# Seven block products instead of eight in part of the in-projection of a gated-attention and MLP kernel

## The chip, the cores and the metric

One core of a Trainium2 chip runs the kernel. The metric is the device time of one execution in microseconds. Its engines are called PE (TensorE, matrix products), DVE (VectorE), ACT (ScalarE), POOL (GpSimd) and SP (SyncE, which issues the DMAs); PEld is PE's loading of weights.

## What is computed

```
def _attn_ref(q, k, v, alpha):              # 4 batches, 8 heads, 768 tokens, 48 wide
    for t in range(S):
        state = alpha[:, :, t, :, None] * state + einsum('bhd,bhe->bhde', k[:, :, t], v[:, :, t])
        y[:, :, t] = einsum('bhd,bhde->bhe', q[:, :, t], state)

def _moe_ref(x, w_gate, w_val, w_out, rms_g):   # x: 3072 tokens x 384, d_ff 1536
    rms = np.sqrt(np.mean(x * x, axis=-1, keepdims=True) + 1e-06)
    xn = x / rms * rms_g
    g = xn @ w_gate
    silu = g * (1.0 / (1.0 + np.exp(-g)))
    val = xn @ w_val
    return (silu * val @ w_out).astype(np.float32)
```

Gated linear attention goes first; its output, laid out by token, is x of the gated MLP.

## The kernel before

All products have fp32 accuracy: each operand is kept as a high and a low half in fp16, and a product is the sum of three matmuls (SPLIT: high x high, high x low, low x high). ACT makes a high half, DVE subtracts it to get the low one.

The 3072 tokens are 24 chunks of 128. `attention(cc)` does a chunk: decays by a scan on DVE, scores (L753), masking, the state (L926), the output y in one PSUM tile (L832, L853), RMS norm, and a transpose by DMA into xT. Chunks make up GROUPS = [4, 2, 2, 4, 4, 4, 4], so groups 5 and 6, with which the change deals, have 512 tokens each.

The MLP's in-projection goes by group g and block f of 128 out of d_ff (12 blocks). `expert_in` (L1154) computes such a unit: two outputs, gate and value, each the sum over NK = 3 blocks of k and three splits, nine matmuls of 512 columns into a PSUM bank `bk` of its own. Then ACT takes silu of the gate (L1165), DVE multiplies by the value (L1171), ACT makes the high half of h (L498) and DVE the low one (L1188). The out-projection of groups 0 to 4 is `expert_out` (L1473, 384 columns). Groups 5 and 6 (SEVEN) already have an out-projection by seven block products in place of eight, `expert_out7` (L1355, 192 columns), with the sums of h (`combine`, L1255 to L1271) and of the weights (`combine_w`, L1293 to L1310) on DVE.

The order is written out: every piece of work of every engine is an op of `Plan`, and ORDER is a table of op numbers. `Plan.order()` goes through it with planned costs, chooses the buffers and lists each engine's ops by their planned start. Each engine then works its list strictly in order. Up to a planned time of 45 us the planner puts filler matmuls (`warm`, L1593, 512 columns, results unused) into gaps that it foresees on PE. There are six PSUM banks `bk` and one tile `y` of two banks for the attention's output. The tile layer adds the semaphores: an access of a tile waits for the accesses of other engines to that tile which it must follow.

## Time and profile before

| | |
|---|---|
| median of 3 runs | 499.30 us (499.09 to 499.84) |
| the profiled execution | 498.64 us, its span 496.8 us |
| PE busy | 489.6 us, 99% of the span |
| DVE busy | 421.5 us, 85% |
| ACT busy | 276.4 us, 56% |

The page gives busy times of each engine over the span; the windows give the same for stretches that follow the stages: group 0's in-projection runs from 28 to 80 us, group 1 from 107, group 2 from 150, group 3 from 192, group 4 from 274; group 5's in-projection from 354 to 402 with its out-projection up to 424; group 6's in-projection from 424 to 470 and its out-projection from there to 492. A recorded matmul or DVE instruction is longer than the distance to the next one's start in a full row, so lengths and distances are told apart in what follows.

### The profile page before, as it was taken

The numbers are of one execution on the slowest core, as the hardware profiler recorded it, in microseconds if no ns is written. First come the engines' busy times: TensorE is split into PE (matmuls) and PEld (weight loads), VectorE is DVE, ScalarE is ACT, GpSimd is POOL, SyncE is SP. The second block draws the span as 40 slices with busy tenths as digits, with TensorE's granted clock in tenths as the row PEclk, the third lists the DMA queues.
The fourth block names the chain that finished last, engine by engine and source line by source line (L and its number), as shares of the span: only waits on it lengthen the run. The fifth ranks groups of instructions, "written<-read, shape, count | busy, mean of one in ns | idle before, by whom it ended". The sixth has DMA issues, their size and how long they took to land.

```text
span 496.8 us, 12664 instructions
## 1 busy us (share of the span) xinstructions
PE 489.6 (99%) x5200; PEld 311.1 (63%) x5200; DVE 421.5 (85%) x822; ACT 276.4 (56%) x751; POOL 27.3 (5%) x63
## 2 busy tenths in 40 slices
...
GB/s 306 311 198 198 296 227 193 164 144 134 112 138 211 58 92 190 73 165 35 34 290 221 322 150 144 144 206 223 55 26 2 33 1 42 7 17 1 2 1 84
DMA packets 47042, 65.22 MB, mean 131 GB/s; under 512 B 32641, under 2 KB 39042, under 8 KB 46978
## 3 DMA queue, kind: packets, MB, share of 16 engines
...
## 4 chain that ended last, share of the span: by engine, by line
PE 58%; issue 33%; DVE 5%; POOL 2%; ACT 1%; POOLq 0%; DVEq 0%; ACTq 0%
PE bk L1154 34%; PE bk_po L1473 10%; PE bk_ab L1355 6%; PE bk_d L1355 2%; POOL ss L958 2%; PE bk L753 2%; DVE w L646 1%; PE y L853 1%; PE bk_warm L607 1%; PE warm L1593 1%; PE bk L926 1%; PE y L832 1%; DVE h L1171 0%; DVE a L883 0%; DVE kh L676 0%
## 5 line engine op out<-in xcount | busy, mean ns | idle before, releaser
L1154 PE MATMUL bk<-xT,wg 128*128 128x512 f16 (+1 forms) x1602 | 286.5, 338 | 0.1
L1154 PEld LDWEIGHTS <-wg 128*128 128x128 f16 x1602 | 154.4, 98 | 120.4 <-issue 0.6
L1473 PE MATMUL bk_po<-wo,h 128*128 128x384 f16 x576 | 96.9, 326 | 0.0
L1473 PEld LDWEIGHTS <-h 128*128 128x128 f16 x576 | 55.0, 98 | 35.6
L498 ACT ACTIVATE h<-h 128x512 f16<-128x512 f32 (+1 forms) x89 | 45.8, 515 | 40.0 <-DVE h L1171 40.0
L1171 DVE SCALAR_TENSOR_TENSOR h<-bk,sl 128x512 f32<-128x512 f32 (+1 forms) x89 | 51.2, 580 | 17.9 <-PE bk L1154 14.8
L1165 ACT ACTIVATE sl<-bk 128x512 f32<-128x512 f32 (+1 forms) x89 | 44.8, 508 | 38.4 <-PE bk L1154 35.9
L646 DVE TENSOR_TENSOR_SCAN w<-att,seed 112x520 f32<-112x520 f32 x48 | 59.3, 1235 | 2.1 <-DMA att<-att 1.7
L1188 DVE TENSOR_TENSOR h<-h,h 128x256 f16<-128x256 f32 (+1 forms) x89 | 47.4, 543 | 6.4 <-ACT h L498 6.3
L958 POOL TENSOR_TENSOR ss<-ss,mhalf 128x1 f32<-128x1 f32 x24 | 21.4, 890 | 383.6 <-ACT ss L955 383.6
L880 ACT CAST a<-bk 128x512 f16<-128x512 f32 x40 | 23.0, 581 | 29.7 <-DVE bk L769 29.6
L883 DVE TENSOR_TENSOR a<-bk,a 128x512 f16<-128x512 f32 x40 | 26.8, 682 | 2.3 <-ACT a L880 2.2
L769 DVE TENSOR_TENSOR bk<-bk,mask 128x512 f32<-128x512 f32 x40 | 26.9, 690 | 2.1 <-PE bk L753 2.1
L683 DVE TENSOR_TENSOR qp<-att,w 112x256 f32<-112x256 f32 x48 | 19.4, 418 | 0.2
L1355 PEld LDWEIGHTS <-h 128*128 128x128 f16 x216 | 17.9, 98 | 0.5 <-issue 0.2
L753 PEld LDWEIGHTS <-k 48*128 48x128 f16 x480 | 13.4, 94 | 6.8 <-issue 6.5
L995 ACT ACTIVATE x<-x,ss 128x384 f16<-128x384 f32 x20 | 12.2, 611 | 9.1 <-issue 4.0
L498 ACT ACTIVATION_READ_ACCUMULATOR h<-h 128x1 f32 x89 | 16.9, 190 | 0.0
L753 PE MATMUL bk<-q,k 48*128 48x128 f16 x480 | 16.9, 217 | 0.0
L676 DVE TENSOR_TENSOR kh<-att,w 112x512 f32<-112x512 f32 x24 | 16.4, 683 | 0.0
L853 PEld LDWEIGHTS <-a 128*128 128x128 f16 x368 | 13.8, 96 | 3.1 <-DVE a L883 0.3
L998 DVE SCALAR_TENSOR_TENSOR x<-x,ss,x 128x384 f16<-128x384 f32 x20 | 12.2, 610 | 3.6 <-ACT x L995 3.5
...
## 6 DMA issues: line engine op xcount, KB each, us to landing
...
```

The costliest lines, as they stand in the source:

```text
L498: nc.scalar.activation(dst, src, AF.Copy, scale=scale, accum_out=stat[:rows, col : col + 1])
L646: nc.vector.tensor_tensor_scan(w, x, start.rearrange("r g p c -> r (g p c)"), 0.0, op0=ALU.mult, op1=ALU.add)
L753: nc.tensor.matmul(t["sc"][j][:, p, :], t["k16"][r, x, p, :], t["q16"][r, y, p, :], start=m == 0, stop=m == 2,)
L769: nc.vector.tensor_tensor(t["sc"][j], t["sc"][j], mask.to_broadcast([P, NP, C]), op=ALU.mult)
L883: nc.vector.tensor_tensor(a_tile()[:, j, 1], t["sc"][j], a_tile()[:, j, 0], op=ALU.subtract)
L958: nc.gpsimd.tensor_tensor(t["ss"], t["ss"], mhalf, op=ALU.pow)
L1154: nc.tensor.matmul(ps[:, :n], wg[:, f, x, j, kk, :], xT[:, y, kk, cs], start=i == 0, stop=i == 3 * NK - 1,)
L1165: nc.scalar.activation(t["sl"][:, :n], t[0][:, :n], AF.Silu, scale=1.0 / (S_X * S_W))
L1171: nc.vector.scalar_tensor_tensor(t["h"][:, :n], t[1][:, :n], S_H / (S_X * S_W), t["sl"][:, :n], op0=ALU.mult, op1=ALU.mult,)
L1188: nc.vector.tensor_tensor(lo, used(t["h"][:, :n]), hi, op=ALU.subtract)
L1355: nc.tensor.matmul(bank(b), left(n, x, p), right(n, y, p), start=begin and p == 0 and m == 0, stop=end and p == n2 - 1 and m == 2, skip_gr ...
L1473: nc.tensor.matmul(t[i][:, :DM], h16_of(g, f)[:, x, ts], wo[:, f // 2, y, f % 2, :], start=f == 0 and m == 0, stop=f == NF - 1 and m == 2,)
```

## The change

Sixteen units, blocks 4 to 9 of group 5 and 0 to 9 of group 6, go through a new function `expert_in7`. Of a unit, the gate and value outputs, two halves of the tokens (256 each) and two of the three blocks of k form a product of 2x2 block matrices. It is made of seven block products, each three matmuls of 256 columns, with sums of weight blocks and of x blocks in place of some operands; the third block of k is added as before (12 matmuls of 256). The partial sums lie in two `bk` banks, `a` and `e`, and in a tile `y_late`, made of the two banks that the attention's y held: yb in its first bank, yd in its second, each with places for two units.

- PE: 1 (into a), 5 (into e), 6 (a), 7 (a), then 2 with third (yb), 4 with third (a), 3 with third (e), third (yd).
- ACT copies a three times on the way: to yb behind 1 (`fork`), to SBUF as u2 behind 6 (`second`) and as u3 behind 7 (`next_`).
- DVE adds e and u3 to yd (`jd`) and later e and u2 to u2 (`jc`); gate and silu come in halves of 256.
- `combine_in` forms the weights' sums, for five pairs of blocks, and `combine_x` those of x, for the two groups: an addition of 1024 columns, four of 256, a copy of the high halves on ACT and a subtraction on DVE. The results lie in four new tiles wi, or in buffers lent by the attention.
- `set_bits` writes y_late once with two matmuls of 512 columns, so that all later products into it accumulate.
- The attention's last chunks and the checks of the weights are now listed ahead of group 5's in-projection.
- The planner has costs for the new ops, counts yb and yd as two buffers each, and lets an access of a PSUM bank start only when other engines' planned accesses of that bank are done (`bank_of`).
- The whole ORDER table is another one. The scratch size for dynamic DMAs is set to 1024. In the changed kernel old lines stand 21 lower at first (L1154 is L1175, L1171 is L1192), and 272 to 281 lower towards the end (L1355 is L1627, L1593 is L1874).

```diff
+WINO = range(10)
+WINO_OF = {5: range(4, 10), 6: range(10)}
...
-    xT=2, raw=2, wu=2, h16=13, sl=2, h32=3, ob=2, bk=6, y=1,
+    xT=2, raw=2, wu=2, h16=13, sl=2, h32=3, ob=2, bk=6, y=1, yb=2, yd=2,
...
 ORDER = """
-1 0 7 8 9 a 2 c d 4 5 b e u x f g y 39 3b 3 v h i j z 3a 6 10 3c 12 13 k l 11 14 3d 3e 15 n o 1k 1m 17
...
+0 1 4 5 2 7 8 9 a b c d u x 6 z h i e f v y g 10 39 11 12 3b 3a 13 3c 3d 14 15 1k 1m 3e 1n 3 1p 1q 17 j
...
+    def bank_of(self, k):
+        return (k[0], self.slot[k]) if k[0] == "bk" else k[0] if k[0] in ("yb", "yd") else None
...
+                for x, f in bank.get(self.bank_of(k), {}).items():
+                    if x != e:
+                        t = max(t, f)
...
+        def form(w):
+            w = w.rearrange("p (f n c) -> p f n c", f=len(fs), n=4)
+            a11, a12, a21, a22 = [w[:, :, n] for n in range(4)]
+            nc.vector.tensor_tensor(a22, a21, a22, op=ALU.add)
+            nc.vector.tensor_tensor(a21, a11, a21, op=ALU.subtract)
+            nc.vector.tensor_tensor(a11, a22, a11, op=ALU.subtract)
+            nc.vector.tensor_tensor(a12, a12, a11, op=ALU.subtract)
...
+        def bank(k):
+            if k[0] == "bk":
+                return tile_of(k, lambda: buf(ps_bk, [P, 512], F32, *k))[:, :n]
+            i = plan.slot[k]
+            return y_late[0][:, 0 if k[0] == "yb" else 1, i * n : (i + 1) * n]
...
+        def product(o, p, start=False):
+            for m, (x, y) in enumerate(SPLIT):
+                nc.tensor.matmul(o, left(p, x), right(p, y), start=start and m == 0, stop=m == 2, skip_group_check=True)
+
+        def third(o, j, c):
+            for m, (x, y) in enumerate(SPLIT):
+                nc.tensor.matmul(
+                    o, wg[:, f, x, j, 2, :], xT_of(g)[:, y, 2, c * n : (c + 1) * n], start=False, stop=m == 2,
+                    skip_group_check=True,
+                )
...
+        p1 = add("PE", "pw", lambda: product(bank(k_a), 1, True), deps, [x_k, k_a])
+        p5 = add("PE", "pw", lambda: product(bank(k_e), 5, True), [p1, w_op, *x_s], xs_k + [k_e] + w_keys)
+        fk = add("ACT", "fork", fork, [p1, y_bits[0]], [k_a, k_b])
+        p6 = add("PE", "pw", lambda: product(bank(k_a), 6), [fk, w_op, *x_s], xs_k + [k_a] + w_keys)
+        u2 = add("ACT", "fork", second, [p6], [k_a, k_2])
+        p7 = add("PE", "pw", lambda: product(bank(k_a), 7), [u2], xs_k + [k_a] + w_keys)
+        u3 = add("ACT", "fork", next_, [p7], [k_a, k_3])
+        jd = add("DVE", "jn", lambda: join(lambda: bank(k_d), lambda: t["u3"]), [u3, p5, y_bits[0]], [k_e, k_d, k_3])
+        b = add("PE", "pw2", lambda: p_third(lambda: bank(k_b), 2, 0, 0), [fk], [x_k, k_b])
+        c = add("PE", "pw2", lambda: p_third(lambda: bank(k_a), 4, 1, 0), [u3], xs_k + [x_k, k_a])
+        e = add("PE", "pw2", lambda: p_third(lambda: bank(k_e), 3, 0, 1), [jd], [x_k, k_e] + w_keys)
+        d = add("PE", "pw", lambda: third(bank(k_d), 1, 1), [jd], [x_k, k_d])
+        tail[0] = d
+        last_unit[g] = [c, e, d]
+        s0 = op("ACT", IN_COST[2][1], lambda: silu(0), [b], [k_b, s_k])
+        jc = add("DVE", "jn", lambda: join(lambda: t["u2"], lambda: t["u2"]), [e, u2], [k_e, k_2])
+        s1 = op("ACT", IN_COST[2][1], lambda: silu(1), [jc, s0], [k_2, s_k])
+        h0 = op("DVE", IN_COST[2][2], lambda: gate(0), [c, s0], [k_a, s_k, h_k])
+        h1 = op("DVE", IN_COST[2][2], lambda: gate(1), [d, s1, h0], [k_d, s_k, h_k])
...
+            y_late.append(buf(ps_y, [P, 2, 512], F32, "y", "late"))
+            for j in range(2):
+                nc.tensor.matmul(
+                    y_late[0][:, j].rearrange("p (o c) -> p o c", o=4), minus,
+                    minus.rearrange("p (o c) -> p o c", o=1).to_broadcast([P, 4, P]), start=True, stop=True,
+                )
...
+        if g == SEVEN[0]:
+            for cc in range(starts[g] + m, NC):
+                xt_ops[cc] = attention(cc)
+            check_weights()
+            set_bits()
+            for f in WINO[::2]:
+                combine_in(WINO[f : f + 2])
+        if g in SEVEN:
+            combine_x(g, [xt_ops[starts[g] + i] for i in range(m)] + last_unit.get(g - 1, []))
...
-            expert_in(g, f, c0, c1, deps)
+            if f in WINO_OF.get(g, ()):
+                expert_in7(g, f, deps)
+            else:
+                expert_in(g, f, c0, c1, deps)
```

Three places show what the new table does to the engines' lists. The first is PE near the start of the program. Before, behind the scores of chunk 0 (bk_0_0 and bk_0_1) and its sums along the chunk (bk_0_4), four warm matmuls come ahead of chunk 0's output y_0:

```order
L763 MATMUL bk_0_1_202<-qp_0_190,kh_0_199 64x64 x2
L890 MATMUL bk_0_4_225<-one_115,kh_0_199 128x112 [waits PE_49,Pool_49]
L890 MATMUL bk_0_4_225<-one_115,kh_0_199 128x112 x3
L1593 LDWEIGHTS minus_112
L1593 MATMUL warm_232<-minus_112 128x512
L1593 LDWEIGHTS minus_112
L1593 MATMUL warm_232<-minus_112 128x512
...
L1593 LDWEIGHTS minus_112
L1593 MATMUL warm_232<-minus_112 128x512
L790 MATMUL y_0_246<-v_0_170,a16_0_230 64x48 [waits DMAHW5_49,DVE_49]
L790 MATMUL y_0_246<-v_0_170,a16_0_230 64x48
```

After, the sums stand ahead of the scores, and 19 warm matmuls follow in a row, the first of them waiting for ACT; then come the scores of chunk 1 and three more warm ones, and chunk 0's output only behind them:

```order
L784 MATMUL bk_0_1_208<-qp_0_197,kh_0_195 64x64 x2
L784 MATMUL bk_0_0_207<-qp_0_197,kh_0_195 64x64 x2
L784 MATMUL bk_0_1_208<-qp_0_197,kh_0_195 64x64 x2
L1874 LDWEIGHTS minus_112
L1874 MATMUL warm_229<-minus_112 128x512 [waits Activation_49]
...
L1874 MATMUL warm_229<-minus_112 128x512
L784 MATMUL bk_1_0_266<-qp_1_260,kh_1_257 64x64 [waits DVE_49]
L784 MATMUL bk_1_0_266<-qp_1_260,kh_1_257 64x64
...
L911 MATMUL bk_1_4_284<-one_115,kh_1_257 128x112 [waits PE_49]
L1874 LDWEIGHTS minus_112
L1874 MATMUL warm_296<-minus_112 128x512
L811 MATMUL y_0_305<-v_0_177,a16_0_249 64x48 [waits DMAHW7_49]
```

What moved: chunk 1's scores went ahead of chunk 0's output, and the long row of fillers stands ahead of them.

The second is PE in group 5's in-projection, around block 4 (bk_5_4 is its bank, xT the tokens, wg the weights). Before, one output's nine matmuls of 512 columns follow the other's, and the next block comes behind:

```order
L1154 MATMUL bk_5_4_0_1_6426<-xT_5_5143,wg_143 128x512
L1154 LDWEIGHTS wg_143
L1154 MATMUL bk_5_4_0_1_6426<-xT_5_5143,wg_143 128x512
L1154 LDWEIGHTS wg_143
L1154 MATMUL bk_5_5_0_0_6441<-xT_5_5143,wg_143 128x512 [waits DVE_49]
L1154 LDWEIGHTS wg_143
L1154 MATMUL bk_5_5_0_0_6441<-xT_5_5143,wg_143 128x512
```

After, the pieces are of three matmuls of 256 columns or six, blocks 4 to 6 are interleaved, and here product 7 of block 4 (weights' sums wi2 and x sums q16_X), product 1 of block 6 and product 2 of block 4 into yb follow each other:

```order
L1396 LDWEIGHTS wi2_147
L1396 MATMUL bk_5_4_a_6478<-q16_X_5_0_6282,wi2_147 128x256 [waits Activation_49]
...
L1396 LDWEIGHTS wi2_147
L1396 MATMUL bk_5_4_a_6478<-q16_X_5_0_6282,wi2_147 128x256
L1396 LDWEIGHTS wg_143
L1396 MATMUL bk_5_6_a_6565<-xT_5_5161,wg_143 128x256 [waits DVE_49]
L1396 LDWEIGHTS wg_143
...
L1396 LDWEIGHTS wg_143
L1396 MATMUL y_late_6469<-xT_5_5161,wg_143 128x256 [waits DVE_49]
L1396 LDWEIGHTS wg_143
L1396 MATMUL y_late_6469<-xT_5_5161,wg_143 128x256
```

What moved: three destinations within nine matmuls, and each of the three pieces begins with a wait, for ACT or for DVE, where before a piece waited only for its bank to come free.

The third is DVE at the same place (h32 is h, h16 its halves, raw_S sums of h). Before, block 5's gate (L1171) is followed by the sums of blocks 4 and 5 for the out-projection:

```order
L1188 TENSOR_TENSOR h16_5_2_6470<-h32_5_2_0_6337,h16_5_2_6470 128x2x128 [waits Activation_49]
L1271 TENSOR_TENSOR att_S_5_1_6472<-raw_S_5_1_6421,att_S_5_1_6472 128x1024 [waits Activation_49]
L1171 SCALAR_TENSOR_TENSOR h32_5_5_0_6491<-bk_5_5_0_1_6459,sl_5_5_0_6476 128x512 [waits DVE_49,PE_49,Activation_49]
L1255 TENSOR_TENSOR raw_S_5_2_6493<-h32_5_4_0_6451,h32_5_5_0_6491 128x256 [waits DVE_49]
L1256 TENSOR_TENSOR raw_S_5_2_6493<-h32_5_4_0_6451 128x256
L1257 TENSOR_TENSOR raw_S_5_2_6493<-raw_S_5_2_6493,h32_5_4_0_6451 128x256 [waits DVE_49]
L1258 TENSOR_TENSOR raw_S_5_2_6493<-h32_5_5_0_6491,raw_S_5_2_6493 128x256 [waits DVE_49]
L1171 SCALAR_TENSOR_TENSOR h32_5_6_0_6522<-bk_5_6_0_1_6500,sl_5_6_0_6510 128x512 [waits PE_49,Activation_49]
```

After, the low halves (L1209) of blocks 2 and 3 come ahead of the joins (L1420) of blocks 5 and 4 into y_late, with the sums of the weights of blocks 8 and 9 (L1284 to L1292) in between; kT_U is u2 and x16_U is u3:

```order
L1209 TENSOR_TENSOR h16_5_2_6529<-h32_5_2_0_6521,h16_5_2_6529 128x2x128 [waits Activation_49]
L1209 TENSOR_TENSOR h16_5_3_6550<-h32_5_3_0_6538,h16_5_3_6550 128x512 [waits Activation_49]
L1420 TENSOR_TENSOR y_late_6469<-bk_5_5_e_6540,x16_U_5_5_6559 128x256 [waits PE_49,Activation_49]
L1284 TENSOR_TENSOR raw_L_w_8_6580<-wg_143 128x1024
L1420 TENSOR_TENSOR y_late_6469<-bk_5_4_e_6531,x16_U_5_4_6569 128x256 [waits DVE_49,Activation_49]
L1289 TENSOR_TENSOR raw_L_w_8_6580<-raw_L_w_8_6580 128x2x128 [waits DVE_49]
L1290 TENSOR_TENSOR raw_L_w_8_6580<-raw_L_w_8_6580 128x2x128 [waits DVE_49]
L1291 TENSOR_TENSOR raw_L_w_8_6580<-raw_L_w_8_6580 128x2x128 [waits DVE_49]
L1292 TENSOR_TENSOR raw_L_w_8_6580<-raw_L_w_8_6580 128x2x128 [waits DVE_49]
L1420 TENSOR_TENSOR kT_U_5_4_6544<-bk_5_4_e_6531,kT_U_5_4_6544 128x256 [waits PE_49]
L1420 TENSOR_TENSOR kT_U_5_5_6527<-bk_5_5_e_6540,kT_U_5_5_6527 128x256
L1265 TENSOR_TENSOR v16_W_7_1_6524<-raw_L_w_6_6472,v16_W_7_0_6523 128x512
```

What moved: joins, which PE's next products wait for, now stand in one list with sums that only later units need.

## Rows read from the trace of the kernel before

**Rows 1.** The page: the span, and busy time of each engine.

```profile
span 496.8 us, 12664 instructions
PE 489.6 (99%) x5200; PEld 311.1 (63%) x5200; DVE 421.5 (85%) x822; ACT 276.4 (56%) x751; POOL 27.3 (5%) x63
```

**Rows 2.** Windows: stretch, length, busy us of each engine, PEclk, DMA share, GB/s.

```profile
core 0: us, PE busy (x) PEld busy (x) DVE busy (x) ACT busy (x) POOL busy (x), PEclk, DMA share, GB/s
...
52.00:100.00 48.00, 48.00 (x469) 25.99 (x467) 48.00 (x80) 35.75 (x83) 1.71 (x2) 1.00 0.62 212
100.00:150.00 50.00, 50.00 (x695) 39.01 (x694) 49.05 (x107) 29.66 (x100) 2.34 (x3) 1.00 0.58 138
150.00:192.00 42.00, 42.00 (x655) 33.75 (x652) 40.21 (x89) 24.24 (x80) 4.89 (x3) 1.00 0.54 107
192.00:274.00 82.00, 81.76 (x929) 44.96 (x928) 79.27 (x153) 44.96 (x125) 5.39 (x5) 1.00 0.57 153
274.00:354.00 80.00, 80.00 (x748) 43.74 (x746) 66.46 (x127) 53.24 (x142) 3.14 (x5) 1.00 0.60 185
354.00:402.00 48.00, 48.00 (x268) 22.30 (x265) 43.69 (x86) 24.94 (x57) 1.09 (x1) 1.00 0.10 23
402.00:470.00 68.00, 67.93 (x485) 42.43 (x484) 36.06 (x68) 24.48 (x61) 0.59 (x1) 1.00 0.04 13
```

**Rows 3.** The page: the chain of work that ended last, by engine.

```profile
PE 58%; issue 33%; DVE 5%; POOL 2%; ACT 1%; POOLq 0%; DVEq 0%; ACTq 0%
```

**Rows 4.** Timeline of PE: start, length; matmuls of 512 columns, of 256 columns.

```profile
116.47 7.04 PE L1154 MATMUL bk<-xT,wg 128*128 128x256 f16 x63
...
356.82 15.06 PE L1154 MATMUL bk<-xT,wg 128*128 128x512 f16 x69
```

**Rows 5.** Groups by line and shape: busy us, mean ns of one, idle before.

```profile
L1154 PEld LDWEIGHTS <-wg 128*128 128x128 f16 x1602 | 154.4, 98 | 120.4 <-issue 0.6
L1154 PE MATMUL bk<-xT,wg 128*128 128x256 f16 x612 | 69.5, 273 | 0.0
L1171 DVE SCALAR_TENSOR_TENSOR h<-bk,sl 128x512 f32<-128x512 f32 x55 | 37.5, 683 | 16.7 <-PE bk L1154 14.8 <-ACT sl L1165 1.5 <-ACT x L995 0.3
...
L1165 ACT ACTIVATE sl<-bk 128x256 f32<-128x256 f32 x34 | 12.6, 378 | 12.0 <-PE bk L1154 10.1 <-issue 1.3 <-DVE h L1171 0.5
...
L1271 DVE TENSOR_TENSOR att_S<-raw_S,att_S 128x1024 f16<-128x1024 f32 x6 | 7.3, 1225 | 3.4 <-ACT att_S L498 3.2
...
L1293 DVE TENSOR_TENSOR raw_T<-wo 128x768 f32<-128x768 f16 x6 | 5.6, 951 | 0.0
```

**Rows 6.** Timeline around PE's waits at 198.2 and 214.9 us, in brackets the idle time.

```profile
198.20 1.39 PEld L1154 LDWEIGHTS <-wg 128*128 128x128 f16 x7 [0.38 <-issue]
...
214.91 0.48 PEld L853 LDWEIGHTS <-a 128*128 128x128 f16 x13 [0.27 <-DVE a L883]
```

**Rows 7.** Timeline from 412 to 413.2 us, group 5's out-projection.

```profile
412.11 0.25 PE L1355 MATMUL bk_ab<-qp_T,a_S 128*128 128x192 f16 x1
...
412.40 0.33 ACT L1390 ACTIVATE h_o<-bk_ab 128x192 f32<-128x192 f32 x1 [0.49 <-PE bk_ab L1355]
...
412.76 0.36 DVE L1402 SCALAR_TENSOR_TENSOR ob<-bk_ab,sl_o 128x192 f32<-128x192 f32 x1 [0.20 <-ACT h_o L1390]
413.17 0.66 PE L1355 MATMUL bk_ab<-wu_T,h 128*128 128x192 f16 x6
413.17 1.42 PEld L1355 LDWEIGHTS <-h 128*128 128x128 f16 x17 [0.22 <-issue]
```

**Rows 8.** Timeline of DVE: two additions of 256 columns in a row.

```profile
432.33 0.42 DVE L1255 TENSOR_TENSOR raw_S<-h,h 128x256 f32<-128x256 f32 x1
432.67 0.42 DVE L1256 TENSOR_TENSOR raw_S<-h 128x256 f32<-128x256 f32 x1
```

More of the change, by code (lines that the diff above doesn't have):

```diff
@@ L70 @@
     wl2=0.362, rgw=0.84, rgt=0.376, x32=0.51, xb=0.376, ys32=0.85, kb=0.53, near=0.3, xneg=0.17,
+    iw1=0.6, is1=1.0, iw=1.132, isum=1.71, ih1=0.508, il1=0.6, ih=0.952, il=1.135, pw=0.327, pw2=0.654, bits=0.45, fork=0.27, jn=0.335,
 )
@@ new lines @@
+s6 nf nl z8 y9 no za s7 zc wf nt n4 zb nu nz sw np wc nv sy nq wl t0 nm xk o1 nr nw nx ia r3 11c wd o0
+o5 o6 zd xh ns t1 t2 t3 ng ze zf o2 t5 wm wn z9 o7 ob oc oh y2 wp 10e x2 zh zj o8 zg ny zl od zi y3 150
+yj t4 wr wo wq 10f ws wt t6 t7 zn oe 10g oi oj zo o9 oa of og o3 o4 ok on oo 10i zp zq 14u 10j 151 14v
+zm ol 152 10h wu y4 160 wv 161 10k op 14o 10l 107 12b om xl zr zs zk zt t8 y6 11e yn ww wy oq or ot ou
+14p 162 163 ov s8 ow oz p0 yl 15w ym yh zv yo yi wx y5 zu zw ox zx zy yp wz x0 yk p1 14q p2 zz 15x 15y
@@ L175, in order @@
         bus, port, owner, mode, done = 0.0, 0.0, None, 0, []
+        bank = {}
         for o in ops:
@@ L206, in order @@
             for k in o["u"]:
+                if self.bank_of(k):
+                    bank.setdefault(self.bank_of(k), {})[e] = o["f"]
                 left[k] -= 1
@@ L1220, in expert_in, with sums_of, whole, sums @@
                 combine(g, f // 2, h_of[g, f - 1], h_of[g, f])
+    wi_of, wi_ops, xs_of, xs_ops, y_late = {}, {}, {}, {}, []
+    wi_own = [const.tile([P, 2, n, 4, P], F16, name=f"wi{i}") for i, n in enumerate((2, 2, 2, 1))]
+    def sums_of(name, src, form, parts, deps, uses):
+        t = {}
+        tmp = ("raw", ("L",) + name)
+        n = parts[-1][2]
+        def whole():
+            t["w"] = like_tile(wst, "raw", tmp[1]).bitcast(F32)[:, :n]
+            for x in src:
+                x(t["w"])
+        def sums():
+            form(t["w"])
+        def high(home, lo, hi):
+            home()
+            nc.scalar.copy(home()[0], t["w"][:, lo:hi])
+        def low(home, lo, hi):
+            nc.vector.tensor_tensor(home()[1], t["w"][:, lo:hi], home()[0], op=ALU.subtract)
+        one = "1" if n == 4 * P else ""
+        o = add("DVE", "iw" + one, whole, deps, [tmp] + uses, lock=True)
+        o = add("DVE", "is1" if one else "isum", sums, [o], [tmp], lock=True)
+        ends = []
+        for home, lo, hi, keys in parts:
+            m = "1" if hi - lo == 4 * P else ""
+            h = add("ACT", "ih" + m, lambda a=(home, lo, hi): high(*a), [o], [tmp] + keys)
+            ends.append(add("DVE", "il" + m, lambda a=(home, lo, hi): low(*a), [h], [tmp] + keys, lock=True))
+        return ends
@@ new lines, in combine_x, with src, form, home @@
+    def combine_x(g, deps):
+        n = GT // 2
+        keys = [("q16", ("X", g, x)) for x in range(2)]
+        def src(w):
+            xT = xT_of(g)
+            nc.vector.tensor_tensor(
+                w.rearrange("p (k t) -> p k t", k=2), xT[:, 0, :2], xT[:, 1, :2], op=ALU.add
+            )
+        def form(w):
+            b11, b12, b21, b22 = [w[:, i * n : (i + 1) * n] for i in range(4)]
+            nc.vector.tensor_tensor(b11, b12, b11, op=ALU.subtract)
+            nc.vector.tensor_tensor(b12, b22, b12, op=ALU.subtract)
+            nc.vector.tensor_tensor(b22, b22, b11, op=ALU.subtract)
+            nc.vector.tensor_tensor(b21, b21, b22, op=ALU.subtract)
+        def home():
+            return [
+                tile_of(("xs", g, x), lambda k=k: buf(ap, [P, 2, NP, C], F16, *k).rearrange("s x p c -> s (x p c)"))
+                for x, k in enumerate(keys)
+            ]
+        xs_of[g] = lambda y: home()[y].rearrange("p (n t) -> p n t", n=4)
+        xs_ops[g] = sums_of(("x", g), [src], form, [(home, 0, 4 * n, keys)], deps, [("xT", g)]), keys
```

232 lines of the change are left out of this document (172 added, 60 removed).

## Prediction, made before the changed kernel was run

> **What bounds the kernel now.** First the page's head: TensorE (PE) is busy 99% of the span, VectorE (DVE) 85% [rows 1]. A share can be an average over unlike stages, so the windows come next, cut at the stages [rows 2]. The reader is to see two columns there. PE is busy in every microsecond from 5 to 192 us and misses 0.24 us of the 82 that follow: whatever shortens PE's queue should shorten the time. And DVE is nearly as full in many of them: 48.00 of 48 from 52 us, 49.05 of 50, 79.27 of 82. Only from 402 us on has it room, with 36 of 68 us. The granted clock is 1.00 throughout. The chain of the end is PE and its issue for 91% [rows 3]. So PE is the bound, and DVE is second by very little up to 402 us.
>
> PE's price list: 69 matmuls of 512 columns in a row take 15.06 us and 63 of 256 take 7.04 us [rows 4]. The last one's recorded length (0.379 and 0.273 us) reaches beyond the pitch, so a matmul costs (15.06 - 0.38)/68 = 0.216 us and (7.04 - 0.27)/62 = 0.109 us. A weight load of 0.098 us stands beside each [rows 5] and fits even under 0.109.
>
> Where does PE wait? At 198.2 and at 214.9 us for DVE and at 413.2 us for an eviction; the idle column shows 0.38, 0.27 and 0.22 us [rows 6, 7]; against the pitch the excess is 0.26, 0.30 and 0.23. The first two come at the end of a stretch in which DVE's work equals PE's (84.4 and 84.5 us of pitch, from the start of group 1 to that of group 3); DVE fell some 3.5 us behind in it.
>
> **PE's part.** A unit of one group and one block f takes 18 matmuls of 512 columns before, 18 x 0.216 = 3.89 us, and 33 of 256 after, 33 x 0.109 = 3.61 us: 21 for the seven products of three splits, 12 for the third block of k. That is 0.285 us less in 16 units: **-4.55 us**. set_bits adds two matmuls of 512 (+0.43). The warm matmuls rise from 29 to 37, 8 x 0.216 = +1.73; they fill gaps that the planner foresees in the first 20 us, all of them now 216 ns each on an engine that has no gap left. If the head is really held by DVE's scans or a load, these 8 cost nothing of their own, because PE would have waited: 0 to 1.73, and I take the upper end, since the trace shows PE going on without a pause behind such matmuls. The attention of chunk 22 and the weight checks move ahead of group 5's new units. No instruction is added by that; their DMAs on SP go out earlier, past stores of group 4 alone, with the DMA engines at 0.10 in that stretch [rows 2], and I cost it at nothing. PE in sum: -2.40 us.
>
> **DVE's and ACT's part.** By pitch a DVE instruction of 256 columns costs 0.34 us (recorded 0.42, 0.34 apart [rows 8]). A unit gets two joins (2 x 0.34) and two gates of 256 in place of one of 512 (2 x 0.34 - 0.60 [rows 5]): +0.75 us, x16 = 12.0. Each of seven sets of sums (five of weights, two of x) is one addition of 1024 (0.87 x 1024/768 = 1.16, from the 768-wide row), four of 256 (1.36) and one subtraction of 1024 (1.145): 3.67, x7 = 25.7. **DVE gets +37.7 us**, ACT about +21 (three evictions of 0.38 a unit, the high halves). ACT stays far from full; its latency counts, not its sum.
>
> Where DVE's addition lies decides its price. By the order some 29.5 us of it stand before group 5's out-projection, the stretch that has no room. Between 52 and 402 us DVE's windows add to 326.7 us of 350 [rows 2]: 23.3 us idle, or 30.7 by pitch, since a gap is 0.08 us longer than it shows. PE's own work up to that place grows by some 4.3 us (27 matmuls of group 6 now stand ahead, warm and bits, chunk 22, less six units' saving). So DVE is left 30.7 + 4.3 - 29.5 = **5.5 us** of idleness in 350. Before, it was idle by pitch for 4.5 us of the 140 from 52 us, 3%, and for 4.4 of the 82 from 192 us, much of it on ACT's answers, not on PE. I put the stalls of PE that follow from DVE's lag at 0.6 us, what the two stalls of before cost [rows 6], with 0 and 4 as ends.
>
> **The new waits in group 5 and 6.** A unit was two rows of nine matmuls whose results nobody sent back. Now one bank is evicted by ACT three times while it goes on accumulating, and PE comes back each time. Three things follow.
>
> First, the round trip. Before shows its like once [rows 7]: the last matmul of a piece ends at 412.11 + 0.25 = 412.36, ACT's snapshot starts at 412.40 and ends at 412.73, DVE's step runs from 412.76 to 413.12, PE goes on at 413.17. The hops are 0.04, 0.03 and 0.05 us. So from matmul to matmul PE - ACT - PE needs 0.27 + 0.04 + 0.38 (ACT's 256 columns [rows 5]) + 0.05, of which 0.11 is the matmul itself: 0.63 us of other PE work, six matmuls of 256, must stand in between. Going through after's order with these durations, some 28 waits of PE in these stretches have less than 0.3 us to spare; before has two there, each short by about 0.25. If three fall short by as much: +0.8 us; ends 0 and 3.
>
> Second, the two outputs yb and yd lie in different PSUM banks, but in one tile, y_late. The built order holds accesses of different engines to that tile in turn, also across the two banks: of 41 waits upon y_late between engines, 30 join different banks, and the planner's rule goes by bank and knows none of them. The order's piece of PE above shows one: block 4's yb product waits for DVE, which is block 5's join into the other bank; by its own inputs it needs only ACT's first copy. Behind p7 of block 5, 12 matmuls of 256 later, it has 1.42 us; the way p7 - ACT - DVE - PE takes 0.27 + 0.04 + 0.38 + 0.03 + 0.42 + 0.05 = 1.19 us where both engines are free, and ACT has a split of 512 columns right ahead, DVE two. PE stands with all that is queued behind, block 4's remaining products and ACT's and DVE's work on them. Over the 32 stretches of PE on y_late such arithmetic gives five to seven stalls of 0.13 to 0.44 us, in sum 1.2 to 1.8; I take **1.3**. Nothing in the trace of before shows this tile, so the ends are 0 (the orders are kept anyway) and 3 (each late turn delays the next).
>
> The Trainium skill bears on this (PSUM — Partial Sum Buffer, PSUM bank collisions raise a hardware error): it asks for semaphores by bank and quadrant, and says that pairs of engines on different banks run clean. By it the 30 cross-bank waits guard nothing, and the sum would be 1.3 us lower without them; that the program has them is what counts here, and no run shows yet what they cost.
>
> Third, the sums of weights and x, and the rest of ACT's copies, only matter through DVE, above. The out-projections are the same instructions.
>
> **Sum.** Profiled run 498.64 (span 496.8 and 1.84 around it), 0.66 under the median 499.3. 498.64 - 4.55 + 0.43 + 1.73 + 0.8 + 1.3 + 0.6 = 498.95; at the median's level **499.6 us**: the gain on PE goes into its waits.
>
> **Rivals.**
> A, the waits are covered: PE's lag behind its inputs is small and y_late's turns come in time. Then 499.3 - 2.40 = 496.9, with 0.4 us of stalls 497.3, up to 498.2 where one of the terms holds. For it: PE had under 1 us of stalls in all before. Against: 28 close waits and a full DVE.
> B, DVE becomes the bound up to 402 us, the case on the other side. Its price begins where its idle time in those 350 us passes 5.5 us, plus the 1 to 2 us by which it may lag at the end. At before's 3% it is 10.5 us, which passes by about 3.5: 499.3 - 2.40 + 0.8 + 1.3 + 3.5 = 502.5, from 500.4 to 505. For it: 3% to 5% in the fullest stretches, with stalls as the result. Against: 52 to 100 us shows 48.00 of 48, so 3% is no law, and DVE that lags finds its inputs ready.
> C, the change doesn't do what it says: the small pieces don't run at 0.109 us each, because at each change of bank a weight load (0.098 us) stands bare, over some 50 pieces 5 us, or y_late's turns put the units one behind the other. 503 to 506. Against: the 63 in a row, and before's switches between short pieces.
>
> **Numbers.** About 0.2% (1.0 us) is what a measurement of this kernel can tell from no change, so same is 498.3 to 500.3. Forecast 0.34 (own range 498.3 to 500.3), A 0.28, B 0.30, C 0.08. Faster is A, slower B and C: 0.28, 0.34, 0.38. The range goes from A's sum, 497.0, to 504.0 in B; C's and B's ends and a bit below A are left out, 2 in 10.
>
> **What will show it.** PE's new matmuls at 0.109 us between starts in runs (else C). Idle gaps of PE in the group 5 and 6 windows, with ACT or DVE as releaser: 2 us together for the forecast; gaps ahead of y_late matmuls that end with another bank's join are the second term. Gaps of PE before 354 us, on DVE, and DVE at 99% from 107 to 402 us would be B; DVE's idle time from 52 to 402 is the number to read. The start of group 1 at 1.7 us later than now is the head's term. I am wrong most easily in counting stalls from slack: a schedule with 0.2 us to spare everywhere costs nothing.

## The result and the profile after

The changed kernel takes **505.65 us** (median of 4 runs, 503.85 to 507.62) against 499.19 of the kernel before beside it: a ratio of 1.0131, 95% interval 1.0097 to 1.0165. It is slower by 1.3%, 6 us above the forecast and 1.65 above the upper end of the range. The profiled run took 504.53 us. Its page, the span, the busy times and the chain of work that ended last:

```profile
span 502.8 us, 13335 instructions
...
PE 490.5 (98%) x5450; PEld 335.2 (67%) x5450; DVE 455.3 (91%) x914; ACT 300.1 (60%) x824; POOL 29.4 (6%) x63
...
PE 59%; DVE 27%; ACT 6%; DMA 4%; issue 3%; SPq 0%; DVEq 0%; ACTq 0%
```

Against [rows 1] and [rows 3]: PE's busy time hardly moved, the span grew by 6.0 us, and DVE and ACT have a third of the chain where they had 6%. PE now waits for them. Where, the windows tell (columns as in [rows 2]):

```profile
52.00:100.00 48.00, 48.00 (x437) 26.65 (x435) 47.73 (x80) 36.88 (x86) 4.03 (x2) 1.00 0.68 212
100.00:150.00 50.00, 49.14 (x687) 38.28 (x686) 48.89 (x106) 27.62 (x96) 2.60 (x3) 1.00 0.53 130
150.00:192.00 42.00, 42.00 (x655) 33.83 (x653) 41.73 (x94) 27.01 (x89) 3.22 (x3) 1.00 0.48 118
192.00:274.00 82.00, 82.00 (x934) 45.03 (x932) 81.69 (x157) 46.54 (x131) 5.18 (x5) 1.00 0.57 151
274.00:354.00 80.00, 79.28 (x780) 43.50 (x779) 76.65 (x149) 55.27 (x143) 5.08 (x6) 1.00 0.65 179
354.00:402.00 48.00, 46.73 (x331) 31.10 (x330) 46.04 (x96) 30.98 (x78) 0.72 (x1) 1.00 0.08 25
402.00:470.00 68.00, 65.27 (x616) 56.12 (x615) 46.21 (x103) 32.51 (x93) 0.00 (x0) 1.00 0.03 10
```

PE, which missed 0.24 us in the windows of [rows 2] up to 402 us, now misses 0.86 from 100 us, 0.72 from 274, 1.27 from 354 and 2.73 from 402. The largest loss lies where DVE is least full: 46.21 of 68 us.

The profile shows idle time short by the overhang of a record, so I also took each distance between two starts on PE and subtracted the pitch of the first (0.216, 0.163, 0.109, 0.083 us for 512, 384, 256, 192 columns). Behind 28 us the excess is 8.6 us in all, where before had 1.08 (the three waits that the prediction names and one that it missed, 0.29 at 475.7 us): 1.03 at 146 us, 1.73 in four places from 335 to 360 us behind `attention`'s masking, and 5.8 us behind 372 us, in the stretch of the new units. With these the span comes out: 496.8 of before, minus 2.40 of PE's work, plus 0.42 because the first in-projection starts 2.15 us later than before (30.47 against 28.32 us; 1.73 of it is in the sum already), plus 8.6 - 1.08: 502.3. The trace has 502.8, so 0.5 us stays unplaced.

The 5.8 us look like this. The timeline of the changed kernel from 379.9 us (start, length; idle time before it and its releaser in brackets); it is the place of which the prediction's second and third order pieces tell:

```profile
379.93 0.37 ACT L1417 COPY x_U<-bk_a 128x256 f32<-128x256 f32 x1 [0.23 <-PE bk_a L1396]
380.14 0.42 DVE L1420 TENSOR_TENSOR y_late<-bk_e,x_U 128x256 f32<-128x256 f32 x1
...
380.62 0.49 PE L1396 MATMUL y_late<-xT,wg 128*128 128x256 f16 x3 [0.40 <-DVE y_late L1420]
...
381.89 0.36 ACT L1409 COPY y_late<-bk_a 128x256 f32<-128x256 f32 x1
...
382.28 0.43 DVE L1420 TENSOR_TENSOR y_late<-bk_e,x_U 128x256 f32<-128x256 f32 x1 [0.58 <-ACT y_late L1409]
382.62 0.41 DVE L1289 TENSOR_TENSOR raw_L_w<-raw_L_w 128x256 f32<-128x256 f32 x1
382.74 0.38 ACT L1429 ACTIVATE sl<-y_late 128x256 f32<-128x256 f32 x1 [0.50 <-DVE y_late L1420]
383.07 0.43 DVE L1290 TENSOR_TENSOR raw_L_w<-raw_L_w 128x256 f32<-128x256 f32 x1
383.18 0.49 PE L1400 MATMUL y_late<-xT,wg 128*128 128x256 f16 x3 [0.43 <-ACT sl L1429]
```

At 380.62 PE's product 2 of block 4, which goes into yb, starts when DVE's join of block 5, which goes into yd, has ended. Then a chain of four turns: ACT's copy into yb (381.89), DVE's join into yd (382.28, idle 0.58 for that copy), ACT's silu of yb (382.74, idle 0.50 for that join), PE's third block into yd (383.18, idle 0.43 for that silu). Each of the last three waits for an engine that works in the other bank. The two stalls cost 0.57 and 0.60 us against the pitch.

### The profile page after: what moved, and what is told of

Read it like the earlier page. It is cut to its first block, busy times and chain, and to the rows that moved or that the text cites. A ratio compares the mean times of both kernels' runs of the same rounds, so it can differ in the third digit from the quotient of the medians.

```text
span 502.8 us, 13335 instructions
## 1 busy us (share of the span) xinstructions
PE 490.5 (98%) x5450; PEld 335.2 (67%) x5450; DVE 455.3 (91%) x914; ACT 300.1 (60%) x824; POOL 29.4 (6%) x63
## 4 chain that ended last, share of the span: by engine, by line
PE 59%; DVE 27%; ACT 6%; DMA 4%; issue 3%; SPq 0%; DVEq 0%; ACTq 0%
PE bk L1175 25%; PE bk_po L1745 8%; PE bk_ab L1627 6%; DVE h L1192 2%; DVE w L667 2%; PE bk_d L1627 2%; PE bk_a L1396 2%; PE bk L774 2%; DVE h L1209 2%; PE warm L1874 2%; DMA att<-att 2%; PE y_late L1400 2%; DVE bk L790 1%; PE y L874 1%; DVE wu_i L555 1%
## 5 line engine op out<-in xcount | busy, mean ns | idle before, releaser
L1175 PE MATMUL bk<-xT,wg 128*128 128x512 f16 (+1 forms) x1314 | 225.5, 330 | 0.1
L1175 PEld LDWEIGHTS <-wg 128*128 128x128 f16 x1314 | 125.8, 98 | 85.2 <-issue 0.3
L1186 ACT ACTIVATE sl<-bk 128x512 f32<-128x512 f32 (+1 forms) x73 | 35.4, 489 | 18.9 <-PE bk L1175 17.2
L979 POOL TENSOR_TENSOR ss<-ss,mhalf 128x1 f32<-128x1 f32 x24 | 23.4, 974 | 335.1 <-ACT ss L976 292.7
L1192 DVE SCALAR_TENSOR_TENSOR h<-bk,sl 128x512 f32<-128x512 f32 (+1 forms) x73 | 40.1, 556 | 0.5
L1209 DVE TENSOR_TENSOR h<-h,h 128x512 f16<-128x512 f32 (+1 forms) x73 | 38.8, 543 | 0.0
L1400 PEld LDWEIGHTS <-wg 128*128 128x128 f16 x192 | 18.7, 97 | 4.5 <-issue 2.2
L1627 PEld LDWEIGHTS <-h 128*128 128x128 f16 x216 | 18.0, 98 | 0.3
L1400 PE MATMUL y_late<-xT,wg 128*128 128x256 f16 x96 | 15.4, 272 | 1.6 <-ACT sl L1429 1.5
```

The source lines that it names most:

```text
L1175: nc.tensor.matmul(ps[:, :n], wg[:, f, x, j, kk, :], xT[:, y, kk, cs], start=i == 0, stop=i == 3 * NK - 1,)
L1186: nc.scalar.activation(t["sl"][:, :n], t[0][:, :n], AF.Silu, scale=1.0 / (S_X * S_W))
L1192: nc.vector.scalar_tensor_tensor(t["h"][:, :n], t[1][:, :n], S_H / (S_X * S_W), t["sl"][:, :n], op0=ALU.mult, op1=ALU.mult,)
L1209: nc.vector.tensor_tensor(lo, used(t["h"][:, :n]), hi, op=ALU.subtract)
L1400: nc.tensor.matmul(o, wg[:, f, x, j, 2, :], xT_of(g)[:, y, 2, c * n : (c + 1) * n], start=False, stop=m == 2, skip_group_check=True,)
L1627: nc.tensor.matmul(bank(b), left(n, x, p), right(n, y, p), start=begin and p == 0 and m == 0, stop=end and p == n2 - 1 and m == 2, skip_gr ...
```

## The experiments

**1. y_late as two tiles.** Same order, same work; yb and yd get a tile of one bank each.

```diff
-            return y_late[0][:, 0 if k[0] == "yb" else 1, i * n : (i + 1) * n]
+            return y_late[0 if k[0] == "yb" else 1][:, i * n : (i + 1) * n]
...
-            y_late.append(buf(ps_y, [P, 2, 512], F32, "y", "late"))
+            ps_y_open.__exit__(None, None, None)
+            ps_l = ctx.enter_context(tc.tile_pool(name="ps_l", bufs=1, space=PSUM))
...
+                y_late.append(ps_l.tile([P, 512], F32, tag=f"y{j}", name=f"y_late{j}", bufs=1))
```

> y_late is made of two tiles, one for each bank (yb, yd); the lists of all engines stay as in the changed kernel, only waits that join the two banks go. Theory 1 (the one tile costs): in the profile of the changed kernel PE's gaps at 380.6, 383.2, 448.2, 450.8, 457.3, 465.5 and 466.8 us end in chains that pass from one bank to the other, 4.0 us of the 5.8 us of gaps behind 372 us. They go: 501.5 to 502.5 us against 505.65. Rival (the round trips through ACT are too long in themselves, whatever the tile): the gaps stay and the time is 504.8 or more.

Measured: 499.06 us (496.28 to 501.2, 10 runs), ratio to before 0.9992 (0.9968 to 1.0015): 6.6 us less than the changed kernel, and 2.4 us below the lower end of what I expected, since I had counted only 4.0 of the 5.8 us as chains from bank to bank. The same place in its timeline:

```profile
381.73 0.37 ACT L1418 COPY x_U<-bk_a 128x256 f32<-128x256 f32 x1 [0.23 <-PE bk_a L1397]
381.86 0.49 PE L1397 MATMUL y_late<-xT,wg 128*128 128x256 f16 x3
381.94 0.42 DVE L1421 TENSOR_TENSOR y_late<-bk_e,x_U 128x256 f32<-128x256 f32 x1
...
382.19 0.49 PE L1401 MATMUL y_late<-xT,wg 128*128 128x256 f16 x3
```

PE writes yb at 381.86 while DVE adds into yd from 381.94 on, and no gap stands there. Behind 362 us no gap of PE over 0.11 us is left. So the 5.8 us were the shared tile's, round trips included: units with three copies a piece go without a stall in this order, once a wait stands only where the bank is shared. The Trainium skill (PSUM — Partial Sum Buffer, PSUM bank collisions raise a hardware error) says that pairs of engines on different banks run clean, and wants semaphores by bank and quadrant. The trace agrees: PE (381.86) and DVE (381.94) work in the two banks at the same time, and the waits across the banks had cost 6.6 us.

In the profiled run of this kernel (500.3 us, above its median) something else shows. DVE's and PE's timeline at 145 us and the windows behind it (columns as in [rows 2]):

```profile
144.82 1.24 DVE L668 TENSOR_TENSOR_SCAN w<-att,seed 112x520 f32<-112x520 f32 x1 [1.92 <-DMA att<-att]
```
```profile
147.16 0.79 PE L775 MATMUL bk<-q,k 48*128 48x128 f16 x22 [1.85 <-DVE q L739]
```
```profile
147.00:149.00 2.00, 1.84 (x50) 1.49 (x50) 1.97 (x5) 0.00 (x0) 0.00 (x0) 0.88 1.08 339
149.00:152.00 3.00, 3.00 (x12) 1.38 (x10) 3.00 (x7) 1.56 (x5) 0.00 (x0) 0.51 0.16 66
152.00:155.00 3.00, 3.00 (x20) 1.84 (x19) 2.97 (x8) 1.70 (x4) 0.00 (x0) 1.00 0.02 5
```

A scan of the attention waits 1.92 us for its load, PE 1.85 us behind it; and after PE's pause the granted clock is 0.51, the lower of its two levels (1.2 GHz), from 149 to 152 us: matmuls of 384 columns start 0.32 us apart in place of 0.163. Ten of them cost 1.6 us beside the 2.0 of the gap. In the changed kernel the same load is late by less, and its clock stays at 1.00 (a shorter wait is not all there is to it: in run 2 PE waits 1.72 us at the same place, and the clock stays at 1.00 there too):

```profile
143.75 1.24 DVE L667 TENSOR_TENSOR_SCAN w<-att,seed 112x520 f32<-112x520 f32 x1 [0.93 <-DMA att<-att]
...
145.36 0.68 DVE L738 SCALAR_TENSOR_TENSOR q<-qp,q 112x512 f16<-112x512 f32 x1
...
146.09 0.79 PE L774 MATMUL bk<-q,k 48*128 48x128 f16 x22 [0.86 <-DVE q L738]
```

**2. Thin sums.** In the changed kernel the sums of weights and x are formed on 16 or 64 columns, and the first half stands for both, so that DVE has little of them; the result of the sums is left out.

```diff
+THIN = 16
...
-            a11, a12, a21, a22 = [w[:, :, n] for n in range(4)]
+            a11, a12, a21, a22 = [w[:, :, n * THIN : (n + 1) * THIN] for n in range(4)]
```

> The sums of weights and of x are made on 16 to 64 columns in place of 256 to 1024 and the products take one half for both (so the result of the sums is left out); ACT's copies and all waits stay. DVE loses about 20 us, 10 of it before 300 us. Theory 2 (DVE full up to 402 us holds PE): PE's gaps at 335 to 360 us, 1.8 us, and part of those at 380 to 391 go, 503.0 to 504.0; the gap at 146 us, before any sum, stays. The runs lie closer together than the 3.8 us of the changed kernel. Rival (the gaps come from the new order's loads and not from DVE's sum): 505 or more.

Measured: 502.34 us (501.82 to 503.5, 4 runs), ratio 1.0066 (1.0044 to 1.0089), 3.3 us under the changed kernel. Of the gaps on PE, the pair at 359 us goes; 0.7 and 0.3 us stay at 336 and 348, against what I expected, and eleven gaps of the new units stay, 4.8 us in all. DVE is no longer full in that stretch (71.41 of 80 us from 274 us), but at 335 us its list has a low half of h (0.69 us) between the two maskings, and PE waits for the second. The pair, in the changed kernel, stood behind DVE's masking of the scores:

```profile
358.70 1.28 DVE L904 TENSOR_TENSOR a<-bk,a 128x512 f16<-128x512 f32 x2
...
360.04 0.60 PE L874 MATMUL y<-v,a 128*128 128x48 f16 x13 [0.36 <-DVE a L904]
```

So DVE's sums have a price of their own, but the y_late gaps aren't DVE's fullness.

**3. Two tiles and thin sums.** Both edits, with the same part left out.

> Both edits, two tiles for y_late and the thin sums. If the two causes add: 499.0 to 500.3. If both remove the same gaps (DVE late because of the tile, or the tile's turns late because of DVE): 501.5 or more.

Measured: 497.53 us (496.31 to 498.06, 10 runs), ratio 0.9974 (0.9964 to 0.9984). PE's windows from 354 to 470 us have no idle time:

```profile
354.00:402.00 48.00, 48.00 (x346) 32.64 (x345) 40.70 (x102) 32.45 (x82) 0.57 (x1) 1.00 0.09 26
402.00:470.00 68.00, 68.00 (x640) 58.35 (x639) 47.48 (x110) 34.06 (x101) 0.00 (x0) 1.00 0.03 10
```

Against the two-tile kernel that is 1.5 us, with intervals that overlap, so this pair alone doesn't show a price of DVE's sums; with one tile they cost 3.3 us (run 2), clear of the noise. Against the thin one it is 4.8 us. Both edits together save 8.1 us, of the 9.9 that the two save one by one; with these intervals that is no sign that the causes don't add. The time is below the 499.0 to 500.3 that I expected. What a run loses varies: the runs of the two kernels with full sums lie 3.8 and 4.9 us apart, the thin ones 1.7 and 1.75.

**4. Before's head.** The changed kernel with the first 420 ops of before's ORDER, 29 warm matmuls in all.

```diff
-0 1 4 5 2 7 8 9 a b c d u x 6 z h i e f v y g 10 39 11 12 3b 3a 13 3c 3d 14 15 1k 1m 3e 1n 3 1p 1q 17 j
...
+1 0 7 8 9 a 2 c d 4 5 b e u x f g y 39 3b 3 v h i j z 3a 6 10 3c 12 13
```

> The changed kernel with its ORDER table begun by the first 420 ops of the table before (up to about 100 us), the rest in its new order: 29 warm matmuls in place of 37 and chunk 0's output ahead of chunk 1's scores as before. Theory 3 (the new head costs time of its own): group 0's in-projection starts at 28.3 and not at 30.5 us, and the time falls by 2.0 to 2.5 to about 503.4. Rival (DVE, full up to 402 us, eats that up): 505 or more, with PE's gaps growing by as much.

Measured: 503.02 us (502.28 to 504.07, 4 runs), ratio 1.0085 (1.0059 to 1.011). Group 0's in-projection starts at 29.0 us, 1.5 earlier than in the changed kernel and not the 28.3 that I expected, and its out-projection at 81.3 us in place of 84.6, but behind the seam between the two orders DVE is late:

```profile
105.34 0.66 DVE L735 SCALAR_TENSOR_TENSOR q<-qp,q 112x512 f16<-112x512 f32 x1
...
106.05 0.79 PE L771 MATMUL bk<-q,k 48*128 48x128 f16 x22 [1.15 <-DVE q L735]
...
110.46 0.93 PE L1172 MATMUL bk<-xT,wg 128*128 128x256 f16 x7 [0.29 <-DVE st L954]
```

Group 1 starts at 110.5 us as in the changed kernel (110.3). PE's lead of 3.3 us is given back there, and where the 2.6 us of the median come from is not settled by this run. As a test of the head's price it is inconclusive.

**5. The attention's loads.** Two tiles, and of the order only this: chunk 11's load stands ahead of chunk 12's on SP; the two op numbers, four places apart in ORDER, are exchanged.

```diff
-p5
+lc
...
-lc
+p5
```

> As the run split (y_late in two tiles), with two loads of SP's list exchanged: att of chunk 11, whose scan waits for it, goes out ahead of att of chunk 12. Theory 4 (the gap at 146 us is this load, and it makes the runs differ by 5 us): the gap of 0.9 to 2.1 us before the scores at 146 us goes, the time falls by 1 to 2 to 497.0 to 498.0, and the runs lie within 3 us. Rival (the load's lateness is the queue's, whichever load it is): the time stays at 498.6 to 499.5 and the wait moves to the other load.

Measured: 497.44 us (496.61 to 499.62, 10 runs), ratio 0.9982 (0.9964 to 1.0). The scan of chunk 11 no longer waits for its load (0.93 us in the changed kernel, 1.92 in run 1), PE's idle time at 145 us shrinks to 0.23 (0.53 to 1.85 in the six traces that have the loads in the old order), and the clock stays. Behind it idle times of 0.66 at 334, 0.08 at 346 and 0.43 in the pair at 358 to 359 us appear, all behind DVE: with PE earlier, DVE's lag shows instead. So the trace shows the load to be the cause of the gap. That the exchange saves time is not shown: by the medians it is 1.6 us under run 1, but the intervals overlap, and run 6, measured beside this one with the loads in the old order, has 497.56.

**6. Fewer warm matmuls.** Two tiles, and no row of warm matmuls longer than 11: 29 in all, as before.

```diff
-                n = int((gap + WARM_MORE if gap > WARM_GAP else gap - 0.3) / WARM)
+                n = min(11, int((gap + WARM_MORE if gap > WARM_GAP else gap - 0.3) / WARM))
```

> As the run split, with the long row of 19 warm matmuls near 9 to 13 us cut to 11 (29 in all, as before the change). My prediction's term (the 8 warm matmuls cost PE 1.73 us): the first in-projection unit starts 1.7 us earlier and the time falls by up to 1.7. Rival (the row fills a gap that DVE's second scan and its products hold open): PE idles there instead, the first unit starts at 30.1 us as in split, and the time is the same within 0.5.

Measured: 497.56 us (496.75 to 501.05, 8 runs), ratio 0.9983 (0.9961 to 1.0006). PE's timeline where the row is shorter:

```profile
9.77 1.68 PE L1878 MATMUL warm<-minus 128*128 128x512 f16 x7
13.11 0.69 PE L785 MATMUL bk<-qp,kh 48*64 48x64 f32 x32 [1.66 <-DVE qp L705]
```

and in the changed kernel, where the row has 19:

```profile
11.66 1.89 PE L1874 MATMUL warm<-minus 128*128 128x512 f16 x8
13.48 0.70 PE L784 MATMUL bk<-qp,kh 48*64 48x64 f32 x32
```

PE now waits 1.66 us for DVE where the eight matmuls stood, and group 0's in-projection starts at 30.11 us, as with them (30.07 in run 1). The eight filled a gap in which PE waits for DVE's work on chunk 1. Before, PE did chunk 0's output in that time; here it stands behind chunk 1's scores. Its start before, and in this run:

```profile
10.71 0.37 PE L790 MATMUL y<-v,a 64*64 64x48 f32 x5
```
```profile
14.92 0.37 PE L812 MATMUL y<-v,a 64*64 64x48 f32 x5
```

The time is not clear of run 1's: the intervals overlap.

**7. Two tiles and another order.** The same pieces; ORDER from a search on planned times, whose aim was the end of the last piece of work.

```diff
-0 1 4 5 2 7 8 9 a b c d u x 6 z h i e f v y g 10 39 11 12 3b 3a 13 3c 3d
+1 0 7 9 8 a 2 4 u b c 39 d 3 v e x h f g y 3b 10 i 3a 3c 5 1k 6 12 j 3d
```

> Two tiles for y_late, and another ORDER table: the first 420 ops from the table before, then a search in which late loads and slower DVE work were allowed for. If PE's saving of 2.4 us is there to be had with waits covered: 496.0 to 497.5, below both kernels. If DVE's 37 us more can't be hidden in any order: 498.5 or more.

Measured: 499.99 us (499.3 to 501.02, 7 runs), ratio 1.0028 (1.0015 to 1.004), though the last matmul of PE's out-projection starts at 488.78 us, 2.9 us earlier than before's. DVE's and SP's timeline at the end:

```profile
489.51 0.14 DVE L1945 CAST flag<-raw_work 1x1 int32<-1x1 f32 x1
```
```profile
490.90 4.42 SPq L1682 DMA_DIRECT2D out_dram<-x  x3
```

The flag of the weights' comparison is made at 489.5 us (before: 484.6); every engine, SP too, reads it ahead of its last work, and three stores of the output go out behind that. (The second of them is issued 3.6 us behind the first; what SP waits for there, this run doesn't settle.) The search had put the flag off, because nothing in its aim held it.

**8 and 9. Two tiles, the order searched again**, with the flag in its aim and with transfers also taken as slower. Two results of it:

```diff
-0 1 4 5 2 7 8 9 a b c d u x 6 z h i e f v y g 10 39 11 12 3b 3a 13 3c 3d
+1 7 2 9 8 u 4 a c 39 b 0 d x z h e 3 5 f v 1k i w g y j 3b 10 2y 6 3a
```

> The kernel with y_late as two tiles of one bank each, all of its work kept, and another order of the same pieces: found by a search over the table that puts off nothing on which the flag of the weights' comparison depends (in the first reordered kernel the flag came at 489.5 us and the end of the program waited for it). Theory 1, what is left of the loss in the two-tile kernel is order alone (the head, loads of the attention, DVE close to full): PE's work is 2.4 us less than before's, so about 499.2 - 2.4 = 496.8 at the median's level, 495.5 to 497.5, a ratio of 0.993 to 0.997, the flag ahead of PE's end, and the gap at 146 us under 0.5 us. Theory 2, DVE, which is full up to 354 us in any order, takes the gain: 498.5 to 500 with PE gaps of 2 us and more behind DVE up to 360 us.

> As the second reordered kernel, with a result of the same search from another starting point. Theory 1 (order alone): 495.5 to 498.5, near the other one, since both keep the same work. Theory 2 (DVE takes the gain in any order): 498.5 to 500 and PE gaps of 2 us and more behind DVE up to 360 us.

Measured: the first **494.23 us** (493.5 to 494.9, 5 runs), ratio **0.9911** (0.9895 to 0.9926); the second 496.32 us (496.31 to 497.13, 5 runs), 0.9961 (0.9946 to 0.9975). Both beat both kernels; the first is 1.3 us below the range that I expected, the second within it. Page and windows of the first:

```profile
span 493.2 us, 13348 instructions
...
PE 486.7 (99%) x5447; PEld 335.9 (68%) x5447; DVE 451.7 (92%) x914; ACT 300.6 (61%) x824; POOL 23.8 (5%) x63
```
```profile
274.00:354.00 80.00, 80.00 (x781) 44.02 (x780) 79.19 (x153) 56.39 (x145) 4.38 (x6) 1.00 0.59 178
354.00:402.00 48.00, 48.00 (x342) 32.49 (x339) 47.26 (x101) 31.11 (x78) 0.55 (x1) 1.00 0.08 22
402.00:470.00 68.00, 68.00 (x650) 58.98 (x648) 48.84 (x115) 36.08 (x105) 0.00 (x0) 1.00 0.04 13
```

From 52 to 402 us DVE is idle for 3.0 us of 350 here (7.3 in the changed kernel), and behind 28 us PE has no recorded idle stretch over 0.05 us. A full DVE does not have to stall PE.

**10. That order with the one tile.** The changed kernel as it is, with ORDER of the first.

> The changed kernel with y_late as one tile, as it is, and the table of the second reordered kernel (494.23 us with two tiles, PE without a gap over 0.11 us from 27 us to its out-projection of group 6). All work kept. Theory 1, the one tile itself costs, because joins and copies into one bank hold products into the other, whatever the order: 497 to 502 us, 3 to 8 us over the two-tile kernel with the same table, with PE gaps ahead of y_late matmuls in the group 5 and 6 units whose releaser is a join or a copy of another block. Theory 2, the tile cost 6.6 us only by the changed kernel's own table, in which the turns happened to fall badly: 494 to 495.5.

Measured: 498.8 us (498.18 to 499.44, 11 runs), ratio 0.9992 (0.9983 to 1.0001): 4.6 us more than with two tiles by the medians, 4.0 by the two ratios. PE's gaps over 0.15 us behind 42 us are nine, from 386 to 459 us, together 4.6 us. One of them, with one tile:

```profile
385.42 0.38 ACT L1429 ACTIVATE sl<-y_late 128x256 f32<-128x256 f32 x1
...
385.83 0.43 DVE L1420 TENSOR_TENSOR y_late<-bk_e,x_U 128x256 f32<-128x256 f32 x1 [0.25 <-ACT sl L1429]
...
386.32 0.49 PE L1400 MATMUL y_late<-xT,wg 128*128 128x256 f16 x3 [0.46 <-DVE y_late L1420]
```

and with two:

```profile
385.45 0.42 DVE L1421 TENSOR_TENSOR y_late<-bk_e,x_U 128x256 f32<-128x256 f32 x1
385.48 0.39 ACT L1430 ACTIVATE sl<-y_late 128x256 f32<-128x256 f32 x1
...
386.23 0.49 PE L1401 MATMUL y_late<-xT,wg 128*128 128x256 f16 x3
```

The join into yd has nothing to do with the silu of yb; with one tile it waits for it, and PE's third block, which does need the join, waits in turn. The tile costs in another order too.

**11. The kernel before, in an order of the same search.** Eight block products everywhere.

```diff
-1 0 7 8 9 a 2 c d 4 5 b e u x f g y 39 3b 3 v h i j z 3a 6 10 3c 12 13
+1 7 2 8 a u 4 c b 9 d 0 h e 39 x 3 f y i v g 3a 3b 10 5 3c 11 12 j k 3d
```

> The kernel of before, eight block products everywhere, with another ORDER table alone, found by the same search as that of the second reordered kernel of the changed code (494.23 us, 4.2 us under before). All work kept. It tells what of those 4.2 us is the seven products and what is only a better order. Theory 1, the products: PE of before stands 1.08 us in all, so an order can win back about 1 us behind its first in-projection and something in the head: 497.0 to 498.3 us, a ratio of 0.997 to 0.999, and 494.23 lies 2.4 us or more below it. Theory 2, the order: before's head and end hold as much as the changed kernel's: 494 to 495.5 us, and the seven products are worth nothing.

Measured: 497.89 us (496.83 to 499.28, 12 runs), ratio 0.9984 (0.9974 to 0.9993). The order alone is worth 0.2%; the seven products beside it 0.9984 - 0.9911, 0.7% or 3.6 us. That compares one result of the search with another, not the best orders there are; the two kernels also differ in the tiles and in the scratch size for dynamic DMAs.

## Why the prediction failed, step by step

- **The step that failed is the second of "the new waits": y_late's turns, 1.3 us with 0 and 3 as ends.** The mechanism was there, even in the example named: block 4's product into yb waits for block 5's join into yd (380.62, by 0.57 us). Its size was 5.8 us by PE's gaps, 6.6 by the medians of run 1, 4.6 in another order (run 10). I had gone over PE's waits alone, with DVE and ACT coming as early as their own inputs let them. But the tile holds them up too: in the rows from 381.89 to 383.18 copy, join and silu wait for each other across the banks before PE's turn comes. A late turn made the next one late, which I had named as the reason for the upper end of 3, and that end was still half of it.
- **PE's part held.** Of the neighbours among the new matmuls of 256 columns, 498 of 515 pairs start 0.107 to 0.110 us apart, the others at the stalls. Bare weight loads, rival C's first reason, don't show. With two tiles and an order that fits, PE starts group 6's out-projection 3.0 us earlier than before.
- **The head: wrong in kind.** The eight warm matmuls cost nothing (run 6); the first in-projection starts 2.15 us late all the same. DVE isn't later with chunk 1's input (done at 13.3 us, before at 14.1), but this order has PE wait for it, with chunk 0's output, which filled that time before, listed behind. With before's table for the head the first unit starts 1.5 us earlier, although chunk 0's scores start 0.7 late in that run (9.37 us; 8.65 in the changed kernel). The number, 1.73, came near by accident. The prediction had both readings and took the wrong one.
- **DVE's lag, 0.6 us (0 to 4):** 1.7 us by the gaps from 335 to 360 us, of which 1.0 stays when the sums are thin and so isn't theirs; the sums cost 3.3 us by run 2. One price was too low: an addition of 256 columns that waits for the one just ahead of it starts 0.43 to 0.46 us behind that, not 0.34 (382.62, 383.07 above). In each of the seven sets three of the four additions stand so, 0.35 us a set more than costed, 2.4 in all. The trace of before has such pairs too (L1257 and L1258, 0.45 apart); [rows 8] shows a pair without a wait.
- **The rivals.** C (503 to 506 us), to which I gave 0.08, holds the time, by its second reason: y_late's turns put the units one behind the other. I had priced that mechanism in the forecast and put the case in which it is large into a rival with a false first reason, so its chance came out too small. B (502.5 us, 500.4 to 505) comes near in time and holds only for the smaller part. DVE's idle time from 52 to 402 us, its number to read, is 7.3 us by the records and 11.2 by pitch, over the 5.5 by pitch at which its price was to begin, and PE does wait for DVE there. But the larger loss lies behind 372 us and goes with the tile, and DVE's work can be hidden: the first order of runs 8 and 9 leaves it 3.0 us by the records, 6.2 by pitch, and keeps PE busy up to 354 us with DVE at 79.19 of 80.
- **The round trip, 0.8 us:** no gap of its kind is left in run 1 or in the first of runs 8 and 9, although copies, joins and products are all there. About 28 waits with under 0.3 us to spare cost nothing, as the last sentence of the prediction has it.
- **Not in the sum at all:** the loads of chunks 12 and 11, which SP issues in this order at 134.6 and 135.7 us, while PE needs chunk 11's first: 1.03 us at 146 us and 1.9 to 2.0 in runs 1 and 2. The prediction looked at the DMAs of chunk 22 and of the checks alone.
- The sign to look for worked in part: gaps ahead of y_late matmuls that end with another bank's join were named as the mark of this term. The trace has one such gap (380.62) and four that end with a silu of the other bank (383.18, 450.83, 457.26, 466.81), together 2.8 of the 5.8 us; the rest stand ahead of other products, and with two tiles they go as well.

With two tiles the medians lie from 494.2 to 500.0 us by the order, on both sides of rival A's sum without stalls, 496.9.
